# A fused attention and MLP kernel: key pieces in pairs, two h units ahead of the third column, and mixed blocks for the last tile but one

## The chip, the cores and the metric

The kernel runs on one core of one Trainium2 chip. The metric is the device time of one execution in microseconds (us). The recorder gives two numbers for each execution: the time, and the span from the first to the last recorded instruction, which is 1.8 us shorter (1196.1 against 1194.3 for the kernel before).

## The reference, cut to what matters

```python
def _attn_ref(u, v, z):                       # u, v: 8 x 3008 x 256, z: 8 x 3008 x 64
    scores = (1.0 / S) * np.matmul(z, z.transpose(0, 2, 1))
    attn = np.maximum(scores, 0.0) ** 2
    return (u * np.matmul(attn, v)).astype(np.float32)

def _moe_ref(x, w_in, w_out):                 # x: 24064 x 256, w_in: 256 x 2048, w_out: 2048 x 256
    h = x @ w_in
    g = h * np.cos(h)
    return (g @ w_out).astype(np.float32)
```

The second function takes the output of the first as its tokens.

## The kernel before

The 24,064 tokens are 48 tiles of 512 (the last of each batch is shorter). Four engines form a pipeline. For a *column* (512 queries of the attention) TensorE multiplies scores into one of the double PSUM banks `E`, ScalarE (ACT) takes the relu, VectorE (DVE) squares it into a *key piece* `A`, and TensorE multiplies the pieces with `v` into two accumulators, one for each half of the 256 outputs: the two `M` banks and one `E` pair. `gate_sum` adds the two row groups of an accumulator (ACT copies one bank, DVE adds the other), and the gate multiplies with `u` to `x`. An *h unit* is four matmuls of x with `w_in` into an `E` bank; ACT takes the cosine `c`, DVE makes `g`. A *y block* is eight matmuls of g with `w_out` into M. From tile 1 to tile 45, y is made from seven *products* of mixed quarters in place of eight plain ones; POOL and DVE add and subtract the quarters.

The order in which the first three columns take their key pieces:

```python
    def phase_a_first(s, n, extra={}):
        ...
        pair = [E[ea][:, 0, :], E[ea][:, 1, :]]
        acc = [pair, M] if s == 1 else [M, pair]
        last = NB - 1
        steps = [
            (dh, k)
            for I in range(NC)
            for dh in range(2)
            for k in range(4 * I, min(4 * I + 4, last))
        ] + [(2, last)]
        lo, hi = 5 if s == 0 else 2, 42      # where the scores of the next column go
        ...
```

The stage that joins h of one tile with y of the tile before it:

```python
    def mixed(m):
        return 1 <= m < NSLOT - 2
    ...
    order_y = (5, 1, 6, 7, 2, 3, 4)
    ...
    def phase_b(s):
        y, hs = s - 2, [(s - 1, i) for i in (0, 4, 1, 5, 2, 6, 3, 7)]
        if s == 2:
            hs = [(0, i) for i in range(8)] + hs
        ...
        if mixed(y):
            ys = [lambda n=n: product(y, n) for n in order_y]
            ...
        else:
            ys = [lambda i=i: emit_y(y, i) for i in range(8)]
            ys[7] = lambda f=ys[7]: (f(), store_y(y))
        n = len(hs)
        if n > 8:
            after = (1, 3, 5, 7, 9, 11, 13, 14)     # y block j follows h unit after[j]
        elif mixed(y):
            ...
```

And the main sequence:

```python
    phase_a_first(0, 12, {4: lambda: turn_late(4), 8: lambda: turn_late(5)})
    phase_a_first(1, 12)
    nc.gpsimd.dma_start(w_out16, moe_w_out.rearrange("(k p) f -> p k f", p=P))
    phase_a_first(2, 14)
    ...
    phase_b(2)
    ...
    for s in range(3, NSLOT + 1):
        ...                                         # phase_a(s) and phase_b(s)
    last_y(NSLOT - 1)
```

Of the kernel before, what the change touches and what calls it, by code (L numbers as in the profile page):

```python
# [14 lines left out]
def kernel(  # L15
# [13 lines left out]
    B, S, D = u.shape  # L29
    dqk = z.shape[2]  # L30
    Dff = moe_w_in.shape[1]
    P = 128
# [3 lines left out]
    NC = (S + CW - 1) // CW  # L36
    WL = S - (NC - 1) * CW
    NFT = Dff // P
    NSLOT = B * NC
# [28 lines left out]
    s1, s2, s4 = (kpool.tile([P, NFT // 2, 2 * P], FP16, name=n) for n in ("s1", "s2", "s4"))  # L68
# [25 lines left out]
    def drop_piece(key):  # L94
        i = pieces.pop(key)
        if pending.get(i):
            pending[i] = "dropped"
        else:
            free_pieces.append(i)
# [247 lines left out]
    def phase_a_first(s, n, extra={}):  # L347
        b, J = s // NC, s % NC
        ea = e_order.pop(0)
        pair = [E[ea][:, 0, :], E[ea][:, 1, :]]  # L350
        acc = [pair, M] if s == 1 else [M, pair]
        last = NB - 1
        steps = [
            (dh, k)
            for I in range(NC)
            for dh in range(2)
            for k in range(4 * I, min(4 * I + 4, last))
        ] + [(2, last)]
        lo, hi = 5 if s == 0 else 2, 42
        at = {}  # L360
        for i in range(n):
            p = lo + (hi - lo) * i // (n - 1)
            at[p] = at.get(p, 0) + 1
        for i, (dh, k) in enumerate(steps):
            if i in extra:
                extra[i]()
            if dh == 2:
                emit_value(b, J, last, 0, 0, acc[0][0], False, True)
                emit_value(b, J, last, 1, 1, acc[1][1], False, True)
            else:  # L370
                for t in range(2):
                    emit_value(
                        b, J, k, t, dh, acc[dh][t], k == 0, k == last - 1 and t != dh
                    )
            if dh > 0 and (k % 4 == 3):
                drop_piece((b, J, k // 4))
                if s > 0:
                    emit_turns((0, 0), 1)
                    if k < 4:
                        turn_u(s)  # L380
                    elif k < 8:
                        for d in range(2):
                            gate_mul(s - 1, d, late_sums.pop(0))
            for _ in range(at.get(i, 0)):
                emit_score(later=squares if s == 0 and i == lo else None)
        if s == 0:
            turn_u(0)
        late_sums.extend(gate_sum(s, *acc[dh]) for dh in range(2))
        hold(late_sums[0][0:1, 0:1])
        load_u(s + 1)  # L390
        e_order.append(ea)
# [4 lines left out]
    def emit_h(m, i):  # L396
        W = mwidth(m)
        x = xs[m]
        e = E[take_e()]
        for f in range(2):  # L400
            ft = 2 * i + f
            for k in range(2):
                nc.tensor.matmul(  # L403
                    e[:, f, 0:W],
                    w_in16[:, k, ft * P:(ft + 1) * P],
                    x[:, k, 0:W],
                    start=(k == 0),
                    stop=(k == 1),
                )
        c = cpool.tile([P, 2, CW], FP16, name="c")  # L410
        nc.scalar.activation(c[:, :, 0:W], e[:, :, 0:W], AF.Sin, bias=half_pi, scale=inv_s2)  # L411
        if m not in gs:
            gs[m] = gpool.tile([P, NFT, CW], FP16, name="g")
        return lambda: nc.vector.scalar_tensor_tensor(  # L414
            gs[m][:, 2 * i:2 * i + 2, 0:W], e[:, :, 0:W], 1.0, c[:, :, 0:W], ALU.mult, ALU.mult
        )

    def mixed(m):
        return 1 <= m < NSLOT - 2

    F = NFT // 2
    T = 2 * P
# [12 lines left out]
    def mix_late(m, which, c):  # L435
        g, f = gs[m], slice(4 * c, 4 * c + 4)
        n, up, low = halves_of(m)
        if which == "s2":
            nc.vector.tensor_tensor(s2[:, f, 0:n], s1[:, f, 0:n], g[:, f, up], ALU.subtract)  # L439
        else:  # L440
            nc.vector.tensor_tensor(  # L441
                s4[:, f, 0:n], g[:, F + 4 * c:F + 4 * c + 4, up], s2[:, f, 0:n], ALU.subtract
            )
# [8 lines left out]
    y_outs, y_parts = {}, {}  # L452

    order_y = (5, 1, 6, 7, 2, 3, 4)
# [6 lines left out]
            )  # L461
        nc.scalar.activation(y_outs[m][0][:, 1, :], acc, AF.Copy, bias=0.0, scale=inv_s2)

    def product(m, n):
        g = gs[m]
        nk, up, low = halves_of(m)
        nk = nk // P
        t = lambda i: w_mix[:, i, :, :]
        left, right = {
            1: (g[:, 0:F, up], w_out16[:, 0:F, 0:P]),  # L470
            2: (g[:, F:, up], w_out16[:, F:, 0:P]),
            3: (s4, w_out16[:, F:, P:D]),
            4: (g[:, F:, low], t(3)),
            5: (s1, t(0)),
            6: (s2, t(1)),
            7: (g[:, 0:F, low], t(2)),
        }[n]
        at = order_y.index(n) + (nk == 1 and n in order_y[4:])
        acc = M[at % 2][:, 0:nk * P]
        for ft in range(F):  # L480
            for k in range(nk):
                nc.tensor.matmul(  # L482
                    acc[:, k * P:(k + 1) * P],
                    left[:, ft, k * P:(k + 1) * P],
                    right[:, ft, :],
                    start=(ft == 0 and k == 0),
                    stop=(ft == F - 1 and k == nk - 1),
                )
        acc = acc.rearrange("p (k d) -> p k d", d=P)
        if n == 5:  # L490
            y_outs[m] = [opool.tile([P, 2, D], FP32, name="o") for i in range(2)]
            y_parts[m] = {}
        c11, c12, c21, c22 = (y_outs[m][i][:, 0:nk, d * P:(d + 1) * P] for i in range(2) for d in range(2))
        parts = y_parts[m]
        add = lambda dst, other: nc.vector.scalar_tensor_tensor(
            dst, acc, inv_s2, other, ALU.mult, ALU.add
        )
        if n in (1, 5, 6):
            parts[n] = ypool.tile([P, 2, P], FP32, name=f"p{n}")[:, 0:nk, :]
        if n in (1, 5):  # L500
            nc.scalar.activation(parts[n], acc, AF.Copy, bias=0.0, scale=inv_s2)
        elif n == 6:
            add(parts[6], parts[1])
            nc.gpsimd.tensor_tensor(c12, parts[6], parts[5], ALU.add)
        elif n == 7:
            add(c21, parts[6])
            nc.gpsimd.tensor_tensor(c22, c21, parts[5], ALU.add)
        elif n == 2:
            add(c11, parts[1])
        elif n == 3:  # L510
            add(c12, c12)
            store_half(m, 0, y_outs[m][0])
        else:
            add(c21, c21)
            store_half(m, 1, y_outs[m][1])

    def y_bank(m, k):
        if m == NSLOT - 1 and k == 3:
            return E[0][:, 0, 0:D]
        return M[k // 2][:, (k % 2) * D:(k % 2 + 1) * D]  # L520

    def y_block(m, ft, k):
        final = m == NSLOT - 1
# [58 lines left out]
    def phase_b(s):  # L582
        y, hs = s - 2, [(s - 1, i) for i in (0, 4, 1, 5, 2, 6, 3, 7)]
        if s == 2:
            hs = [(0, i) for i in range(8)] + hs
        for dh in range(len(late_sums)):
            gate_mul(s, 2 - len(late_sums), late_sums.pop(0), nc.gpsimd)
        if mixed(y):
            ys = [lambda n=n: product(y, n) for n in order_y]
            if mwidth(y) < CW:  # L590
                ys.insert(4, lambda: middle(y))
        else:
            ys = [lambda i=i: emit_y(y, i) for i in range(8)]
            ys[7] = lambda f=ys[7]: (f(), store_y(y))
        n = len(hs)
        if n > 8:
            after = (1, 3, 5, 7, 9, 11, 13, 14)
        elif mixed(y):
            after = (0, 1, 2, 3, 4, 5, 6, 6)
        else:  # L600
            after = (0, 1, 2, 3, 4, 5, 6, 6)
        for i, (m, unit) in enumerate(hs):
            times_c = emit_h(m, unit)
            if not mixed(y):
                times_c()
            for f, place in zip(ys, after):
                if place == i:
                    f()
            if mixed(y):
                times_c()  # L610
            if mixed(m) and unit >= 4:
                mix_early(m, unit - 4)
            if i in (1, 3, 5):
                emit_turns((0, 0), 1)
# [58 lines left out]
    M = [ppool.tile([P, CW], FP32, name=f"M{i}", tag=f"M{i}") for i in range(2)]  # L673
# [26 lines left out]
    phase_a_first(0, 12, {4: lambda: turn_late(4), 8: lambda: turn_late(5)})  # L700
    phase_a_first(1, 12)
    nc.gpsimd.dma_start(w_out16, moe_w_out.rearrange("(k p) f -> p k f", p=P))
    phase_a_first(2, 14)
    assert done_groups[0] == need[3]
    emit_turns((0, 3))
# [63 lines left out]
```

## Time and profile before

| | before |
|---|---|
| time | 1197.23 us, median of 3 runs (1196.8 to 1197.61) |
| profiled run | 1196.1 us, span 1194.3 us |
| TensorE busy | 1184.6 us of the span, 99% |
| next busiest | DVE, 1008.6 us, 84% |

The prediction shows the head of the page and the stops between 36 and 56 us. Three other places are needed to follow the argument. In the timelines the columns are: start in us, duration in us, engine, line, operation, output and inputs, shapes, count; in brackets the idle time before it and what ended it. This is the timeline of TensorE of the kernel before, around 24 us, where column 1 begins:

```profile
24.47 0.59 PE L258 MATMUL M<-A,v 64*128 64x512 f16 x3 [0.28 <-DVE sm L270]
25.07 0.39 PE L194 MATMUL E<-zT 64*128 64x512 f16 x2
```

Two things wait there for the same engine: the value matmul into M, and then, in order, a score that needs an E bank. DVE's own timeline in the same window shows who lets the score go:

```profile
24.34 0.68 DVE L270 TENSOR_TENSOR sm<-E,sm 128x512 f32<-128x512 f32 x1
```

It ends at 25.02, and the score starts at 25.07. The third place is the last stage, 8 h units of tile 47 with 8 y blocks of tile 46; the first and last lines of it in the timeline of TensorE of the kernel before:

```profile
1168.92 1.03 PE L403 MATMUL E<-xodd,w_in 128*128 128x512 f16 x4
1169.79 1.04 PE L524 MATMUL M<-w_out,g 128*128 128x256 f16 x8
...
1182.82 1.36 PE L524 MATMUL M<-w_out,g 128*128 128x256 f16 x11
```

It takes 13.89 us and TensorE never stops in it.

### The profile page before, as it was taken

Reading aid. Unit: us, or ns where it says so; the run is one execution under the profiler, and the core shown is the slowest. Engines: PE = TensorE matmul, PEld = TensorE weight load, DVE = VectorE, ACT = ScalarE, POOL = GpSimd, SP = SyncE. Lnnn points to the kernel's source line nnn. Section 1 sums busy time; section 2 is a strip of 40 time slices with the busy share of each in tenths; the row PEclk is TensorE's granted clock in tenths of the full one; section 3 lists DMA queues with packets and bytes.
Section 4 is the critical chain, followed back from the end, with each engine's and each line's share of the span. In section 5 each row is a group of like instructions: output and inputs, shape, how many; then the busy total and the mean of one; then the engine's idle time right before and its main releaser. Section 6 shows DMA issues by size and latency. Waiting matters only on the chain.

```text
span 1194.3 us, 28924 instructions
## 1 busy us (share of the span) xinstructions
PE 1184.6 (99%) x11839; PEld 727.2 (61%) x11839; DVE 1008.6 (84%) x1293; ACT 795.1 (67%) x927; POOL 678.4 (57%) x707
## 2 busy tenths in 40 slices
PE   9899999999999999999999999999999999999998
PEld 4556655665566656566556665666656666665566
DVE  6798988888988898888988889888888888888775
ACT  7866666666766676666766676766766666666454
POOL 3186745557565573665647556476565765545450
PEclk9999999999999999999999999999999999999999
DMA  9999898769995699956999459974798838954301
GB/s 159 172 165 163 121 153 127 118 107 137 139 139 104 114 140 157 128 92 113 150 147 132 91 107 156 169 117 77 121 160 154 122 70 122 183 105 89 65 19 54
DMA packets 479861, 147.98 MB, mean 124 GB/s; under 512 B 404208, under 2 KB 479472, under 8 KB 479728
## 3 DMA queue, kind: packets, MB, share of 16 engines
q1 hardware_dynamic: 380752, 112.93, 54.5%
q0 software_dynamic: 97440, 32.78, 28.1%
q8 instruction: 92, 1.51, 0.5%
q10 hardware_dynamic: 1536, 0.43, 0.2%
q14 instruction: 41, 0.34, 0.1%
HBM read 66.32 MB, written 24.64 MB: 76 GB/s over the span
## 4 chain that ended last, share of the span: by engine, by line
PE 97%; ACT 1%; DVE 1%; issue 1%; ACTq 0%; DVEq 0%
PE E L403 27%; PE M L482 23%; PE M L258 20%; PE E L258 19%; PE E L194 5%; PE M L524 2%; ACT r L204 1%; PE M L459 1%; PE E L654 0%; DVE sm L270 0%; PE E L524 0%; DVE A L209 0%; DVE x L286 0%; DVE g L414 0%; PE M L677 0%
## 5 line engine op out<-in xcount | busy, mean ns | idle before, releaser
L411 ACT ACTIVATE c<-E 128x1024 f16<-128x1024 f32 (+1 forms) x384 | 385.6, 1006 | 218.0 <-PE E L403 214.8
L414 DVE SCALAR_TENSOR_TENSOR g<-E,c 128x1024 f16<-128x1024 f32 (+1 forms) x384 | 458.9, 1197 | 66.7 <-ACT c L411 65.7
L204 ACT ACTIVATE r<-E 128x512 f16<-128x512 f32 (+1 forms) x342 | 327.8, 967 | 114.1 <-PE E L194 108.4
L258 PEld LDWEIGHTS <-v 64*128 64x128 f16 x4512 | 246.8, 94 | 232.4 <-issue 20.6
L403 PE MATMUL E<-x,w_in 128*128 128x512 f16 (+1 forms) x1408 | 353.8, 375 | 0.0
L432 POOL TENSOR_TENSOR s<-g 128x512 f16<-128x512 f16 (+1 forms) x180 | 202.9, 1127 | 185.4 <-DVE g L414 138.9
L258 PE MATMUL M<-A,v 64*128 64x512 f16 (+1 forms) x2256 | 284.9, 372 | 2.1 <-ACT sm L269 1.2
L258 PE MATMUL E<-A,v 64*128 64x512 f16 (+1 forms) x2256 | 279.4, 372 | 0.0
L433 POOL TENSOR_TENSOR g<-g 128x512 f16<-128x512 f16 (+1 forms) x180 | 214.2, 1190 | 14.1
L403 PEld LDWEIGHTS <-w_in 128*128 128x128 f16 x1536 | 133.4, 98 | 108.6 <-issue 19.1
L482 PEld LDWEIGHTS <-g 128*128 128x128 f16 x2752 | 168.6, 98 | 39.8
L209 DVE TENSOR_TENSOR A<-r 128x1024 f16<-128x1024 f16 x240 | 173.3, 734 | 15.1 <-ACT r L204 14.3
L286 POOL TENSOR_TENSOR x<-sm,uT 128x512 f16<-128x512 f32 (+1 forms) x43 | 48.5, 1130 | 214.1 <-DVE sm L270 213.9
L482 PEld LDWEIGHTS <-s 128*128 128x128 f16 x2064 | 126.6, 98 | 30.6
L194 PE MATMUL E<-zT 64*128 64x512 f16 (+4 forms) x684 | 130.0, 356 | 0.5 <-ACT zT L647 0.3
L439 DVE TENSOR_TENSOR s<-s,g 128x1024 f16<-128x1024 f16 (+1 forms) x90 | 98.5, 1094 | 2.1 <-POOL s L432 2.1
L482 PE MATMUL M<-w_out,g 128*128 128x128 f16 x1376 | 91.5, 219 | 0.0
L482 PE MATMUL M<-w_mix,g 128*128 128x128 f16 x1376 | 91.5, 219 | 0.0
L482 PE MATMUL M<-w_mix,s 128*128 128x128 f16 x1376 | 91.5, 219 | 0.0
L212 DVE TENSOR_TENSOR A<-r 128x512 f16<-128x512 f16 (+1 forms) x102 | 80.7, 792 | 10.2 <-ACT r L204 9.4
L194 PEld LDWEIGHTS <-zT 64*128 64x128 f16 x684 | 39.3, 94 | 36.7 <-issue 2.2
L441 DVE TENSOR_TENSOR s<-g,s 128x1024 f16<-128x1024 f16 (+1 forms) x90 | 59.4, 662 | 0.0
(58 smaller groups left out, 657.6 us busy)
## 6 DMA issues: line engine op xcount, KB each, us to landing
out_dram<-o SPq DMA_DIRECT2D x87, 256.0 KB, 2.2
v<-in_v_dram POOLq DMA_DIRECT2D x40, 256.0 KB, 9.2
u<-in_u_dram POOLq DMA_DIRECT2D x40, 256.0 KB, 4.8
A<-A SPq DMA_TRANSPOSE x252, 5.2
z<-in_z_dram POOLq DMA_DIRECT2D x14, 192.0 KB, 10.6
z<-in_z_dram POOLq DMA_DIRECT2D x14, 176.0 KB, 6.3
v<-in_v_dram POOLq DMA_DIRECT2D x8, 192.0 KB, 12.0
u<-in_u_dram POOLq DMA_DIRECT2D x8, 192.0 KB, 4.0
```

Source lines behind the costliest of these rows:

```text
L194: nc.tensor.matmul(e[:, t, 0:Wt], zT[rows, k * P:(k + 1) * P], zT[rows, J * CW:J * CW + Wt], start=True, stop=True,)
L204: nc.scalar.activation(r[:, :, 0:W], e[:, :, 0:W], AF.Relu)
L209: nc.vector.tensor_tensor(a4, r4, r4, ALU.mult)
L212: nc.vector.tensor_tensor(a4, r[:, :, 0:W], r[:, :, 0:W], ALU.mult)
L258: nc.tensor.matmul(bank[:, 0:width(J)], vs[b, k // 4][t * H:(t + 1) * H, k % 4, dh * P:(dh + 1) * P], value_rhs(b, J, k, t), start=start, ...
L403: nc.tensor.matmul(e[:, f, 0:W], w_in16[:, k, ft * P:(ft + 1) * P], x[:, k, 0:W], start=(k == 0), stop=(k == 1),)
L411: nc.scalar.activation(c[:, :, 0:W], e[:, :, 0:W], AF.Sin, bias=half_pi, scale=inv_s2)
L414: return lambda: nc.vector.scalar_tensor_tensor(gs[m][:, 2 * i:2 * i + 2, 0:W], e[:, :, 0:W], 1.0, c[:, :, 0:W], ALU.mult, ALU.mult)
L432: nc.gpsimd.tensor_tensor(s1[:, f, 0:n], g[:, f, low], g[:, lower, low], ALU.add)
L433: nc.gpsimd.tensor_tensor(g[:, f, low], g[:, f, up], g[:, f, low], ALU.subtract)
L439: nc.vector.tensor_tensor(s2[:, f, 0:n], s1[:, f, 0:n], g[:, f, up], ALU.subtract)
L482: nc.tensor.matmul(acc[:, k * P:(k + 1) * P], left[:, ft, k * P:(k + 1) * P], right[:, ft, :], start=(ft == 0 and k == 0), stop=(ft == F - ...
```

## The change

Its intent: take away the stops of TensorE at both ends of the program. Part 1 lets each accumulator of columns 1 and 2 take eight key blocks in turn and not four, so the second accumulator is touched later. Part 2 issues two of the sixteen h units of the first joint stage ahead of column 2, where TensorE waits for the M banks. Part 3 makes y of tile 46 from seven products too. The core of the diff (cut: the plumbing that passes each product its place, and the swap of the two M banks for the last tile):

```diff
+        run = 1 if s == 0 else 2
         steps = [
             (dh, k)
-            for I in range(NC)
+            for I in range(0, NC, run)
             for dh in range(2)
-            for k in range(4 * I, min(4 * I + 4, last))
+            for k in range(4 * I, min(4 * (I + run), last))
         ] + [(2, last)]
...
     def mixed(m):
-        return 1 <= m < NSLOT - 2
+        return 1 <= m < NSLOT - 1
...
-            hs = [(0, i) for i in range(8)] + hs
+            hs = [(0, i) for i in range(2, 8)] + hs
...
-            ys = [lambda n=n: product(y, n) for n in order_y]
+            late = s == NSLOT
+            ys = [
+                lambda n=n, i=i: product(y, n, i)
+                for i, n in enumerate((1, 5) + order_y[2:] if late else order_y)
+            ]
...
-            after = (1, 3, 5, 7, 9, 11, 13, 14)
+            after = (1, 2, 4, 5, 7, 8, 10, 11)
+        elif s == NSLOT:
+            after = (0, 1, 3, 4, 5, 6, 7)
...
+            if s == NSLOT and i in (1, 3):
+                for c in range(2):
+                    mix_late(y, "s2" if i == 1 else "s4", c)
...
     phase_a_first(1, 12)
     nc.gpsimd.dma_start(w_out16, moe_w_out.rearrange("(k p) f -> p k f", p=P))
+    for i in range(2):
+        emit_h(0, i)()
     phase_a_first(2, 14)
```

More of the change, by code (lines that the diff above doesn't have):

```diff
@@ L462, in middle, with product @@
         nc.scalar.activation(y_outs[m][0][:, 1, :], acc, AF.Copy, bias=0.0, scale=inv_s2)
-    def product(m, n):
+    def product(m, n, place):
         g = gs[m]
@@ L477, in product @@
         }[n]
-        at = order_y.index(n) + (nk == 1 and n in order_y[4:])
-        acc = M[at % 2][:, 0:nk * P]
+        acc = M[(place + (nk == 1 and place >= 4)) % 2][:, 0:nk * P]
         for ft in range(F):
@@ L489, in product @@
         acc = acc.rearrange("p (k d) -> p k d", d=P)
-        if n == 5:
+        if m not in y_outs:
             y_outs[m] = [opool.tile([P, 2, D], FP32, name="o") for i in range(2)]
@@ L519, in y_bank @@
             return E[0][:, 0, 0:D]
-        return M[k // 2][:, (k % 2) * D:(k % 2 + 1) * D]
+        bank = 1 - k // 2 if m == NSLOT - 1 else k // 2
+        return M[bank][:, (k % 2) * D:(k % 2 + 1) * D]
     def y_block(m, ft, k):
```

## The prediction

> **What bounds the kernel now.** I read the page first. TensorE (PE) is busy 1184.6 of 1194.3 us and no other engine is above 84%; the chain of work that ended last says the same:
>
> ```profile
> PE 1184.6 (99%) x11839; PEld 727.2 (61%) x11839; DVE 1008.6 (84%) x1293; ACT 795.1 (67%) x927; POOL 678.4 (57%) x707
> ...
> PE 97%; ACT 1%; DVE 1%; issue 1%; ACTq 0%; DVEq 0%
> ```
>
> The reader is to see that time can come from two sources only: PE work removed, or the 9.7 us in which PE stands still. The steady middle (columns 3 to 46) is the same instruction sequence before and after, buffers aside, as a comparison of the two built programs shows. So the ends of the program decide. The timeline of PE, windows 35 to 41 and 51 to 58 us, has the two largest stops outside the start-up:
>
> ```profile
> 37.69 0.37 PE L258 MATMUL M<-A,v 64*128 64x512 f16 x1 [1.22 <-ACT sm L269]
> 38.65 0.80 PE L258 MATMUL M<-A,v 64*128 64x512 f16 x5 [0.59 <-DVE sm L270]
> ...
> 52.05 1.90 PE L403 MATMUL E<-x,w_in 128*128 128x512 f16 x8
> 55.52 1.05 PE L524 MATMUL M<-w_out,g 128*128 128x256 f16 x8 [1.58 <-DVE g L414]
> ```
>
> Column 1 ends at about 36.3 us; column 2 begins in the two M banks, which ACT (L269) and then DVE (L270) must read first. By start times PE loses 37.69-36.31 = 1.38 and 38.65-37.91 = 0.74 us, 2.1 us together. At 52.05 the first two h units of tile 0 are issued, and the first y block needs their g, which DVE has only at 55.46: 55.52-53.77 = 1.75 us lost. Matmul ends are modelled, so I count starts, not the bracketed idle time. A third, small stop is in the timeline at 74 to 76 us:
>
> ```profile
> 73.99 1.08 ACT L554 ACTIVATE o<-M 128x512 f32<-128x512 f32 x2
> 74.70 0.10 PEld L258 LDWEIGHTS <-v 64*128 64x128 f16 x2 [0.42 <-issue]
> 74.70 1.87 PE L258 MATMUL M<-A,v 64*128 64x512 f16 x12
> 75.12 0.95 PEld L258 LDWEIGHTS <-v 64*128 64x128 f16 x10 [0.33 <-issue]
> ```
>
> Column 3 writes M while ACT still copies y of tile 0 out of it (to 75.07): about 0.3 us lost.
>
> **What the Trainium skill says.** (1) "TensorE: Matmul & The Clock Gate", section "Wait — 56ns, not 53.3ns?": a warm matmul of N columns starts N/2.4 GHz + about 2.5 ns after the one before, 215.7 ns at N=512. The trace agrees: h, h, y repeats every 2.60 us (56.41, 59.01, 61.61), which is 8 x 0.2157 + 8 x 0.109. So an h unit (4 matmuls of 512) and a y block (8 of 256) each cost 0.866 us of PE, and a mixed product (16 of 128) 0.89 (h plus product repeat every 1.755 us). (2) The same page, section "The mechanism": matmuls are strict FIFO. So one blocked matmul stops all behind it, and moving an independent h unit ahead of the blocked one is a gain. (3) "SBUF — State Buffer", section "Who interferes with whom": a DVE op with two SBUF inputs contends with a GpSimd op that reads SBUF, one with a single SBUF input does not. The trace agrees: the mixing sums of L439 take 0.69 us alone and 1.64 beside POOL, while L414, which reads PSUM and c, stays at 1.22 us. That matters for part 3.
>
> **The change part by part.**
>
> *Part 1, key pieces in pairs in columns 1 and 2.* No matmul is added or removed. In column 1 (dh=0 in an E pair, dh=1 in M) M is first touched at step 8, no longer step 4. That removes the 0.28 us stop at 24.47. But the score matmul after step 5 needs an E bank that the DVE sum frees at 25.02, and it starts at 25.07 before; it is still the next thing on PE, with the same wait. So PE arrives early and stops at the same 25.07: gain 0. The reordering needs squares earlier (row piece 3 at step 20 and not 24); they land at 29.25 for a use at about 29.6 us in column 1, so I expect no new stall.
>
> *Part 2, two h units ahead of column 2.* Their inputs are there: x of tile 0 at 30.5, w_in landed at 13.98+11.2 = 25.2 us. They run from 36.31 to 38.04, inside the hole; the second M bank frees at about 38.6 as before. So 2 x 0.866 = 1.73 us of PE work vanish from after column 2. In exchange ACT has two sines (1.94 us) and DVE two g products ahead of column 2's scores. Column 2 has one E pair as accumulator, so its scores alternate on the same two E's that h used. The first can start when DVE is through with g 0: 38.6+1.2 = 39.8, not 39.09; the second at 41.0, not 39.96. ACT's chain of 14 relus, unbroken before (39.70 + 12.61), starts its second 1.0 us later; there is 0.2 to 0.3 us of slack until the narrow score at 46. I take column 2 to end 0.9 us later, at 52.95.
>
> Then two h's (units 2 and 3) to 54.7, then the first y block, whose g is long there. What it waits for now is w_out: issued at 39.31, 16.0 us to landing by the table of DMA issues, so 55.3. It begins at about 55.4, against 55.52. From there the kernel before had 14 h and 8 y, 22 x 0.866 = 19.05 us (55.52 to 74.6, as the trace shows); now it is 12 h and 8 y, 17.3 us. DVE has 14 g products at a pitch of 1.14 to 1.22 us, 16 to 17 us from 55.4, and the new spacing (three h, two y in 4.33 us) leaves it keeping up. Gain 1.73 + 0.12 = 1.85 us. The last y is now followed by two h units (1.73 us of PE) where one was, so ACT's copies of M (1.08 us) are over before column 3: gain another 0.3.
>
> *Part 3, y of tile 46 in seven products.* Before: 8 y blocks and 8 h units, 1168.92 to 1182.82 = 13.9 us. Now 8 h and 7 products: 8 x 0.866 + 7 x 0.89 = 13.16, a gain of 0.74 on PE alone. But no score column runs in this stage, so the mixing sums come inside it. Walking through it: the last g of tile 46 is ready at 1171.4, POOL's sum s1 at about 1172.6 to 1172.8, and the second product would need it at 1172.2: 0.5 us lost. DVE gets 8 g products (1.14 pitch), 4 sums (0.61), 5 additions (0.34): about 13.3 us from 1171.4 on, so DVE ends near 1185.0, just ahead of the last matmuls that need its g. PE then reaches the last tile at about 1182.6, 0.25 us earlier. The two output buffers of tile 46 are stored earlier than the last tile needs them, so the tail is unchanged. Gain 0.25.
>
> Sum: 1.85 + 0.3 + 0.25 + 0 = 2.4 us. 1197.23 - 2.4 = **1194.8 us**.
>
> **The rivals.**
> 1. *w_out lands earlier or does not gate.* If it lands before 54.7, y starts when PE gets there and the gain of part 2 is up to 2.6, the total 3.2: 1194.0. For it: transposes share the DMA engines and might move. Against: its issue is tied to the same DVE sum (38.59), and the software queue is busy until about 55.
> 2. *The E banks, not M, become the wait of column 2.* If relus stay late through the column by more than 1 us, or the two g products delay squares that column 2 multiplies with, part 2 gives back 0.5 to 1 us more: 1195.5. For it: ACT had no idle time there before. Against: y waits for w_out until 55.4 anyway, which hides the first 0.7 us.
> 3. *DVE becomes the bound of the last stage.* It had 10.68 of 13.90 us there; now it is near full. If POOL's share or the additions stretch it by 0.5 us, part 3 costs 0.3 where I gain 0.25: 1195.4.
> 4. *Column 3 runs into POOL.* POOL's mixing for tile 1 ends at about 82.7 us by its own chain, while column 3 comes 2 us earlier; DVE sums then sit beside POOL longer (1.64 for 0.69). If M or E is freed late, 0.5 to 1 us goes: 1195.5. Against: I find the second sum's input at 81.2, about when DVE gets there.
>
> **Range and chances.** All of the parts act on 50 of 1194 us, and all PE idle time outside start-up is below 5 us, so 2% (24 us) either way is out of reach short of a hang-like wait. The rivals span 1194.0 to 1196; the runs before differ by 0.8 among themselves. Range 1193.7 to 1196.3. Faster by over 2%: 0.01; within 2%: 0.98; slower: 0.01.
>
> **What would show it.** In the new profile: two L404 groups at about 36.3 without a stop before 38; the first scores of column 2 waiting for DVE at 39.8 and 41.0; the first L525 matmul at 55.4, waiting for w_out's DMA and not DVE; column 3 starting near 72.6 with no stop after its first step; the step at 25.07 unchanged; a short wait on POOL in the second product of the last stage and DVE almost full there; last-tile matmuls 2.1 + 0.25 us earlier than 1182.82. The prediction is wrong if column 2 ends past 53.7, if y starts after 56, or if the middle is not shifted by a constant of about 2.1 us.

## The result, and the profile after

| | before | after |
|---|---|---|
| time, median (range), 4 runs each | 1197.01 us (1196.61 to 1197.61) | 1193.32 us (1192.88 to 1193.59) |
| profiled run | 1196.1 us, span 1194.3 | 1193.15 us, span 1191.4 |

The ratio is 0.9968, 95% interval 0.9951 to 0.9986. It is "same" by the 2% line, as predicted, but the time lies 0.4 us below the range and the median moved by 3.7 us, not 2.4.

The head of the page of the changed kernel:

```profile
PE 1183.3 (99%) x11887; PEld 727.2 (61%) x11887; DVE 1012.3 (85%) x1302; ACT 794.9 (67%) x927; POOL 690.5 (58%) x717
...
PE 97%; ACT 1%; DVE 1%; issue 0%; POOL 0%; DVEq 0%; ACTq 0%
```

48 more matmuls, 1.3 us less busy time on TensorE, and the same engine ends last. The spans differ by 2.95 us, so by this count more than half of the gain is stops taken away and not work; as matmul ends are modelled, the starts below decide. The timeline of TensorE of the changed kernel in the hole that the prediction is about:

```profile
36.30 1.90 PE L404 MATMUL E<-x,w_in 128*128 128x512 f16 x8
38.13 1.21 PE L258 MATMUL M<-A,v 64*128 64x512 f16 x6
39.77 0.39 PE L194 MATMUL E<-zT 64*128 64x512 f16 x2 [0.43 <-DVE g L415]
...
40.90 0.39 PE L194 MATMUL E<-zT 64*128 64x512 f16 x2
```

The eight h matmuls fill the hole; the price is the scores at 39.77 and 40.90 (39.09 and 39.96 before), which wait for the g products. Behind column 2, in the same view:

```profile
52.77 1.90 PE L404 MATMUL E<-x,w_in 128*128 128x512 f16 x8
54.51 1.04 PE L525 MATMUL M<-w_out,g 128*128 128x256 f16 x8
```

The first y block follows the two h units with no bracket, so with no stop: 54.51 - 52.77 is two h units of 0.87. Before, the same two lines stood at 52.05 and 55.52. The weights `w_out` that this block needs were issued at 39.2 and had landed at 54.1, just in time (view of the tile `w_out`, changed kernel):

```profile
L712 POOL DMA_DIRECT2D w_out<-in_moe_w_out_dram x1: 1159/1159/1159, 39.2 to 39.2; - x1
...
DMA to landing us min/median/max: 14.9/14.9/14.9
```

Where column 3 begins, ACT's copies of y are now done before TensorE comes (timeline of all engines, changed kernel):

```profile
70.37 1.08 ACT L555 ACTIVATE o<-M 128x512 f32<-128x512 f32 x2
71.95 1.47 PE L258 MATMUL M<-A,v 64*128 64x512 f16 x12
```

The score near 25 us still waits for the same sum of DVE, only its bracket is longer, as the work ahead of it went faster:

```profile
24.96 0.39 PE L194 MATMUL E<-zT 64*128 64x512 f16 x2 [0.66 <-DVE sm L270]
```

And the last stage has two new stops (timeline of TensorE, changed kernel):

```profile
1168.64 0.83 PE L482 MATMUL M<-w_mix,s 128*128 128x128 f16 x12
1169.80 0.40 PE L482 MATMUL M<-w_mix,s 128*128 128x128 f16 x4 [0.32 <-POOL s L433]
1170.03 1.89 PE L404 MATMUL E<-xodd,w_in 128*128 128x512 f16 x8
1171.78 1.22 PE L482 MATMUL M<-w_mix,s 128*128 128x128 f16 x16
1172.84 1.03 PE L404 MATMUL E<-xodd,w_in 128*128 128x512 f16 x4
```

A product of 16 matmuls takes 0.89 us where nothing stops it. The first shown here, which is the second product of the stage, takes 1.39 (to 1170.03), the next 1.06 (to 1172.84): 0.5 and 0.17 us lost.

Cutting both traces at the start of the same matmuls gives where the time went:

| stretch, by starts of matmuls | before | after | difference |
|---|---|---|---|
| to the score near 25 us | 25.07 | 24.96 | -0.11 |
| columns 1 and 2, to the h units after column 2 | 26.98 | 27.81 | +0.83 |
| to the first y block | 3.48 | 1.74 | -1.74 |
| to column 3 | 19.18 | 17.44 | -1.74 |
| column 3 | 11.63 | 11.23 | -0.40 |
| first h after column 3 to first h after column 4 | 25.08 | 25.34 | +0.26 |
| from there to the last stage | 1057.51 | 1057.51 | 0 |
| last stage | 13.89 | 13.84 | -0.05 |
| sum | | | -2.95 |

The two profiled runs differ by 1196.1 - 1193.15 = 2.95 us as well, so nothing is left over between them. But the medians differ by 3.7. The sum of the prediction was 2.4. There were thus two questions: which terms were mis-sized in the pair of traces (0.55 us), and why the medians differ by 0.7 us more than the traces.

### The profile page after: what moved, and what is told of

Same layout as the page of the kernel before. It is cut to its first block, busy times and chain, and to the rows that moved or that the text cites. A ratio compares the mean times of both kernels' runs of the same rounds, so it can differ in the third digit from the quotient of the medians. Undisturbed runs are those within 1.5% of the kernel's fastest.

```text
span 1191.4 us, 29044 instructions
## 1 busy us (share of the span) xinstructions
PE 1183.3 (99%) x11887; PEld 727.2 (61%) x11887; DVE 1012.3 (85%) x1302; ACT 794.9 (67%) x927; POOL 690.5 (58%) x717
## 4 chain that ended last, share of the span: by engine, by line
PE 97%; ACT 1%; DVE 1%; issue 0%; POOL 0%; DVEq 0%; ACTq 0%
PE E L404 27%; PE M L482 23%; PE M L258 20%; PE E L258 19%; PE E L194 5%; PE M L525 1%; ACT r L204 1%; PE M L460 1%; DVE g L415 0%; PE E L664 0%; DVE sm L270 0%; PE E L525 0%; POOL s L433 0%; ACT c L412 0%; DVE o L495 0%
## 5 line engine op out<-in xcount | busy, mean ns | idle before, releaser
L433 POOL TENSOR_TENSOR s<-g 128x512 f16<-128x512 f16 (+1 forms) x184 | 208.3, 1132 | 188.5 <-DVE g L415 138.7
L434 POOL TENSOR_TENSOR g<-g 128x512 f16<-128x512 f16 (+1 forms) x184 | 219.5, 1193 | 14.4
L482 PEld LDWEIGHTS <-g 128*128 128x128 f16 x2816 | 172.5, 98 | 40.8
L482 PEld LDWEIGHTS <-s 128*128 128x128 f16 x2112 | 129.4, 98 | 32.1 <-DVE s L440 0.5
L194 PE MATMUL E<-zT 64*128 64x512 f16 (+4 forms) x684 | 127.6, 355 | 2.0 <-DVE sm L270 0.7
L482 PE MATMUL M<-w_mix,s 128*128 128x128 f16 x1408 | 94.0, 219 | 0.3 <-POOL s L433 0.3
```

What stands on the lines that cost most here:

```text
L194: nc.tensor.matmul(e[:, t, 0:Wt], zT[rows, k * P:(k + 1) * P], zT[rows, J * CW:J * CW + Wt], start=True, stop=True,)
L433: nc.gpsimd.tensor_tensor(s1[:, f, 0:n], g[:, f, low], g[:, lower, low], ALU.add)
L434: nc.gpsimd.tensor_tensor(g[:, f, low], g[:, f, up], g[:, f, low], ALU.subtract)
L482: nc.tensor.matmul(acc[:, k * P:(k + 1) * P], left[:, ft, k * P:(k + 1) * P], right[:, ft, :], start=(ft == 0 and k == 0), stop=(ft == F - ...
```

## The experiments

Fourteen runs of ten kernels were made in four sets, each set on one chip beside runs of the kernel before. All outputs are right. The traces repeat to about 0.02 us in most stretches; what varies from run to run is the start, the landing of `w_out`, and one thing that the first set brought up.

### Each part alone, and the change again

`p1_only` has only the first hunk of the diff (`run`). `p2_only` has only the two h units, their removal from the later list, and the new `after`. `p3_only` is the changed kernel with those two parts undone. `after_again` is the changed kernel.

> Key pieces in pairs alone (part 1). Theory A (the gain is the two h units in the hole, as the two traces show it): 0, within 0.2 us of before; the score matmul near 25 us still waits for the DVE sum, and the first y block still waits for g near 55.5. Rival B (the new order of the pieces moves the transposes and so the landing of w_out, and that made the part of the gain that I had not foreseen): still 0 here, since g gates y as well, but w_out lands at about 54.1 and not at 55.3. Rival C (part 1 removes a stop of its own): 0.3 to 0.7 us faster.

> Two h units ahead of column 2 and the new spacing alone (part 2). Theory A: nearly the whole gain, 2.7 to 3.7 us, and the first y block starts at about 54.5 us with w_out landed before it. Rival B: w_out lands at about 55.3 as in the trace of before, the first y block waits for it, and the gain is 0.7 to 0.9 us smaller than that of the whole change.

> y of the last but one tile in seven products alone (part 3). Theory A (the stage lost in waits on POOL and DVE what it gained in matmuls): 0 to 0.2 us faster, with the wait of 0.5 us on POOL in the second product and 0.35 us on the DVE sum in the third. Rival: 0.7 us faster, as the matmul count says, the difference in the profiles of the pair being chance.

> The changed kernel unchanged, on the same chip as the three others. The spans of the first pair of profiles differ by 2.9 us and the timed medians by 3.7. Theory A: the middle is the same to 0.01 us in all runs, so that the difference is chance in when the first inputs and w_out arrive; several spans of both kernels give 3.0 to 3.6 us. Rival: a gain of 3.7 us or more, which would mean that the profile of before was a lucky run in which a wait was shorter than usual.

| | median us (range), 5 runs | ratio to before, 95% |
|---|---|---|
| before, 9 runs | 1197.57 (1195.87 to 1198.22) | |
| p1_only | 1197.66 (1195.91 to 1197.77) | 0.9996 (0.9982 to 1.0009) |
| p2_only | 1193.09 (1193.01 to 1194.78) | 0.9968 (0.9956 to 0.9981) |
| p3_only | 1196.16 (1195.86 to 1196.46) | 0.999 (0.9977 to 1.0002) |
| after_again | 1193.46 (1192.88 to 1194.53) | 0.9969 (0.9957 to 0.9982) |

Part 2 alone gives the whole gain. Part 1 gives nothing: the score near 25 us starts at 25.05 in its trace, and column 1, from its first value matmul to its last, takes 13.38 us there as in the kernel before. Part 3 makes the last stage 13.84 us, as in the changed kernel, and leaves all stretches ahead of it as before; its median looks 1.4 us better only because all five of its runs lie in the lower of the two groups, about 1.5 us apart, into which the runs of the kernel before fall, so that is no effect of it.

Two surprises. First, in `after_again` the first y block came at 56.05 and not 54.51 (timeline of TensorE):

```profile
52.98 1.90 PE L404 MATMUL E<-x,w_in 128*128 128x512 f16 x8
56.05 1.05 PE L525 MATMUL M<-w_out,g 128*128 128x256 f16 x8 [1.17 <-ACT c L412]
```

The bracket names ACT, whose cosine was long done; the table of transfers has `w_out` landing 16.6 us after its issue at 39.4, at 56.0. So it is the transfer. Second, `p1_only` changes nothing near 40 us, and yet its stretch "columns 1 and 2" took 28.51 us and not 26.98. The windows view shows why. The columns are the stretch, its length, the busy time (instructions) of PE, PEld (weight loads), DVE, ACT and POOL, the granted clock (the share of TensorE's full speed that the trace records), the DMA share and GB/s. The kernel before:

```profile
36.00:39.00 3.00, 1.20 (x11) 0.41 (x7) 2.21 (x4) 1.64 (x3) 0.60 (x2) 1.00 1.22 216
39.40:43.20 3.80, 3.80 (x39) 2.14 (x36) 2.00 (x3) 3.50 (x4) 1.07 (x1) 1.00 0.99 124
```

The trace of `p1_only`:

```profile
36.00:39.00 3.00, 1.20 (x10) 0.41 (x7) 2.19 (x4) 1.61 (x3) 0.63 (x2) 1.00 1.23 212
39.40:43.20 3.80, 3.80 (x24) 1.70 (x20) 1.39 (x2) 2.23 (x3) 1.05 (x1) 0.55 0.99 132
```

TensorE is as busy, but does 24 matmuls where 39 went, at a mean clock of 0.55. The recorded grant is 0.5 for one interval of 3413 ns, from 39.6 to 43.0 us. It comes right behind the hole at 36 to 38.6, where TensorE did almost nothing (1.20 us of 3.00: the end of column 1, one matmul at 37.67, and the first of column 2 from 38.62). Value matmuls start 0.43 us apart in it and not 0.215, and the stretch is 1.53 us longer. So a new theory, called H: **the hole of the kernel before makes the clock halve for one interval in some of its runs, and the h units that fill the hole also take this away.** Its rival R: those slower runs have some other cause, and the changed kernel has them as well.

### Is the hole to blame for the slower runs?

`before_look`, `before_look2` and `before_look3` are the kernel before, to catch the slower group in a trace. `before_fill` and `before_fill2` are the kernel before with eight matmuls of no use in the hole:

```diff
+    for i in range(8):
+        nc.tensor.matmul(E[e_order[0]][:, 0, :], warm[:, 0:P], warm, start=True, stop=True)
     phase_a_first(2, 14)
```

> The kernel before with eight matmuls of zeros (8 x 0.216 = 1.73 us, results never read) in the hole between columns 1 and 2, and nothing else. They do no useful work and fit into a stop that is there anyway. Theory H (the hole of 2.3 us lets the throttle halve the clock for one window of 3.4 us in about two runs of three, as the trace of part 1 alone shows from 39.6 to 43.0; that costs 1.5 us and makes the upper group of the spans of before, 1195.8 to 1196.4 beside 1194.1 to 1194.8): all spans in the lower group, median 1196.0 to 1196.5, so 1.0 to 1.5 us faster than before. Rival R (the two groups come from when w_out or the first inputs land): the same as before within 0.3 us, with both groups still there.

> The kernel before again, for its trace only. Theory H: if its span is above 1195.5 us, its trace shows matmuls at half rate for 3.4 us after the hole at 36 to 38.6 us; if it is below 1195, it shows none. Rival R: a long span without such a stretch, its first y block later than 55.5 us and behind w_out.

> The kernel before, for its trace. Theory H: a span above 1195.7 us shows matmuls at half rate for 3.4 us after the hole near 36 to 38.6 us, and the stage from the score at 25 to the first h unit takes 28.5 us and not 26.98; a span below shows 26.98. Rival R: a long span with 26.98 us in that stage.

> As the look before: Theory H: a span above 1195.7 us with 28.5 us from the score at 25 to the first h unit, or a span below with 26.98. Rival R: a long span with 26.98.

> The kernel before with the eight idle matmuls in the hole, again: the first time the before runs beside it were nearly all in the lower group (8 of 11), so that nothing could be gained, and one run of 1200.8 us spoilt the mean. Theory H (the hole causes the halved clock): no span between 1195.7 and 1196.6 us; in ten runs of the two jobs at most the lone far one, against 8 of 29 in before. Rival R (the halved clock comes whatever is in the hole): 2 of 5 spans in the upper group.

`before_look` (span 1194.7 us) and `before_look3` (1194.6) fell in the lower group, with no throttled interval. `before_look2` (1197.46 us, span 1195.7): its windows view reads like that of `p1_only`, and nothing in the kernel differs from the profiled run of before:

```profile
36.00:39.00 3.00, 1.20 (x11) 0.42 (x8) 1.99 (x4) 1.42 (x3) 0.82 (x2) 1.00 1.24 214
39.40:43.20 3.80, 3.80 (x24) 1.68 (x20) 1.39 (x2) 2.48 (x3) 0.85 (x1) 0.55 0.98 126
```

All its other stretches agree with before to 0.01 us; columns 1 and 2 take 28.51 for 26.98. In the two traces of the slower group that exist, the halved clock thus makes the difference. All six traces of kernels with the hole open fit: two with a halved interval and spans of 1195.7 and 1195.9, four without and spans of 1194.1 to 1194.7.

In the four sets, 12 of 38 runs of the kernel before have a span of 1195.6 or more (5 of 9, 3 of 11, 0 of 9 and 4 of 9). With the hole filled by useless matmuls, none of 10 runs lies there (the highest is at 1195.5, just short of it), against 7 of 20 runs of before beside them; an eleventh run of `before_fill`, at a span of 1200.8 us, is unexplained. No median moved: `before_fill` 1196.79 us (1196.25 to 1202.65) for 1196.4 of before, ratio 1.0008 (0.9993 to 1.0024); `before_fill2` 1196.65 (1196.49 to 1196.75) for 1196.63, ratio 0.9998 (0.9985 to 1.001). Where the expectation was that the median would fall, it was missed: most runs of before are in the lower group anyway, so the median sits there; what the filling changed is the upper end of the range, 1196.75 for 1197.74 us in the second set. For H speak the traces and the missing upper group; the counts alone are too few to prove it. None of the eight traces with h units in the hole has the interval.

The record holds two more checks. It gives the mean granted clock of every run, traced or not. One halved interval loses 1.7 us of clock, so a run that has one can't be listed at 1.000. All 12 long runs of the kernel before are listed at 0.999 or 0.998; of the 26 others, 23 are at 1.000. This is a sign and no proof, as some clock is also lost behind the last matmul (up to 1.2 us in the traces). The filled run at 1195.5 is at 1.000, so it has no halved interval. The one at 1200.8 is at 0.997, a loss of 3 us or more: either its clock halved although the hole was filled, or its end was long; no trace shows which.

The second check is where the stop lies. In every trace the full clock is first granted between 3.9 and 7.2 us, and both halved intervals begin ten steps of 3.413 us after that; so the steps can be counted off in all traces. The stop lasts 2.34 us and begins between 36.1 and 36.7. In the two halved traces it lies whole within one step (36.19 to 39.60 in `p1_only`, 36.04 to 39.45 in `before_look2`). In the four others with the hole open, a step ends inside the stop (at 37.07, 37.94, 37.02 and 38.08; in the last, `p3_only`, 2.0 us of the stop lay in one step, and the clock stayed full). In `before_fill` (step 35.80 to 39.21) and four traces with h units in the hole (`after`, `after_third`, `after_late_order`, `best`), a step covers the place whole, matmuls fill it, and the clock stays full. An estimate from these figures: if the steps fall evenly, a stop of 2.34 us lies whole within one in (3.41 - 2.34) / 3.41 = 31% of the runs, and 12 of 38 is 32%. So where the stop falls among the steps seems to decide whether a run is slow. This fits all eleven traces, but no run set the position on purpose.

### Does w_out gate the first y block?

`after_wout_early` issues the load one column earlier:

```diff
+    nc.gpsimd.dma_start(w_out16, moe_w_out.rearrange("(k p) f -> p k f", p=P))
     phase_a_first(1, 12)
-    nc.gpsimd.dma_start(w_out16, moe_w_out.rearrange("(k p) f -> p k f", p=P))
```

`after_third` is the changed kernel a third time, to see whether its runs ever show the halved clock or the wait.

> The changed kernel with w_out issued one column earlier, right after column 0. In the changed kernel w_out landed at 54.1, 54.9 (part 2 alone) and 56.0 us in three profiles, and the first y block, ready at about 54.5, waited 0.0, 0.4 and 1.5 us for it. Theory: w_out lands before 50 us, no wait, and the upper runs (1194.4 to 1194.8) are gone: median 1192.9 to 1193.2, all runs within 0.8 us. Rival (the upper runs come from elsewhere, or the earlier transfer delays the transposes or v): same or slower, spread as before.

> The changed kernel again, so that three jobs show how often it waits for w_out. Theory: spans of 1191.1 to 1191.8 without the wait, up to 1193.0 with it (1 to 2 of 5), none with the halved clock in column 2. Rival: the long spans come from a halved clock here too, and the trace, if it is a long one, shows it.

`after_wout_early`: 1193.14 us (1192.86 to 1193.27), ratio 0.997 (0.9958 to 0.9982), spans 1191.0 to 1191.5. Its load lands after 11.3 us, long before it is needed, and the first y block follows 1.74 us after the h units. `after_third`: 1193.05 us (1192.82 to 1193.76), ratio 0.9967 (0.9953 to 0.998); its trace (span 1192.0) names the wait outright, in the timeline of TensorE:

```profile
52.96 1.90 PE L404 MATMUL E<-x,w_in 128*128 128x512 f16 x8
55.34 1.05 PE L525 MATMUL M<-w_out,g 128*128 128x256 f16 x8 [0.48 <-DMA w_out<-in_moe_w_out_dram]
```

So the wait that the prediction named exists, but not in every run. In the fourteen traces with the load in its old place it lands 14.1 to 16.6 us after issue; of six with the h units ahead, three wait for it (`p2_only` 0.3, `after_third` 0.64, `after_again` 1.3 us) and three do not. Taking it away cost nothing here and makes runs alike; the median hardly moves (the changed kernel's lie between 1193.05 and 1193.46).

### What the seven products gave back

`after_late_order` keeps the seven products of the last stage, but orders them so that those which need the sums of POOL and DVE come later:

```diff
-                for i, n in enumerate((1, 5) + order_y[2:] if late else order_y)
+                for i, n in enumerate((1, 2, 5, 6, 7, 3, 4) if late else order_y)
...
-            after = (0, 1, 3, 4, 5, 6, 7)
+            after = (0, 1, 2, 4, 5, 6, 7)
```

> The changed kernel with another order of the seven products of tile 46: the two that need no mixed block first, the sums later (1, 2, 5, 6, 7, 3, 4, the empty place after the fourth h unit). Theory (part 3 gained 0.06 instead of 0.74 us because the second and third product wait 0.5 us for POOL and 0.3 us for DVE): these waits vanish and the stage is 0.6 to 0.8 us shorter; median 0.5 to 0.8 us below the changed kernel. Rival (DVE is the bound of this stage, at 10.7 us of g products, 2.6 of sums and 1.7 of additions in 13.9): no gain, the wait appears in front of the last tile's matmuls.

It ran 1192.88 us (1192.31 to 1193.38), ratio 0.9969 (0.9956 to 0.9982); the last stage is 13.30 us, 0.54 less than with the changed kernel's order. That is somewhat less than the 0.6 to 0.8 us expected, and the median is 0.2 to 0.6 us below those of the changed kernel, taken in other sets. Its timeline of TensorE has, where the two stops were, none:

```profile
1170.00 1.06 PE L482 MATMUL M<-w_mix,s 128*128 128x128 f16 x16
1170.89 1.89 PE L404 MATMUL E<-xodd,w_in 128*128 128x512 f16 x8
1172.62 1.06 PE L482 MATMUL M<-w_mix,s 128*128 128x128 f16 x16
1173.51 1.03 PE L404 MATMUL E<-xodd,w_in 128*128 128x512 f16 x4
```

Both products take 0.89 us. So the work saved by the seven products is real, and the order gave it back. The wait for POOL was the reason and not, as rival 3 had it, DVE as the bound of the stage: DVE has the same work here and the stage is shorter. DVE is now close to being the bound, though: the windows view has it busy for 12.85 us of the 13.30.

### What column 3 gained

The second matmul of the first pair of column 3 starts 0.42 us after the first in before (ACT still copies M), at once in the changed kernel. `after_old_space` puts the last two y blocks later, so that the copies end later:

```diff
-            after = (1, 2, 4, 5, 7, 8, 10, 11)
+            after = (1, 3, 5, 7, 9, 11, 12, 12)
```

> The changed kernel with the y blocks of tile 0 spaced as before (one after every second h unit), so that only one h unit follows the last y block. By the stages of its trace: Theory (the new spacing saves the stop at the start of column 3, in which the second of two paired matmuls waits 0.42 us for ACT's copy of M and the pairs stay apart to the end of the column): column 3 takes 11.6 us again and not 11.22, all other stages as in the changed kernel. Rival (column 3 is shorter because DVE is less behind): 11.2 us.

It ran 1193.03 us (one look, span 1191.2). The copies now end 0.1 us after column 3 starts (timeline of all engines):

```profile
70.91 1.08 ACT L555 ACTIVATE o<-M 128x512 f32<-128x512 f32 x2 [0.51 <-PE M L525]
...
71.88 1.61 PE L258 MATMUL M<-A,v 64*128 64x512 f16 x12
```

The second matmul trails by 0.16 us, and column 3 takes 11.37 us, between the 11.63 of before and the 11.22 of the changed kernel. That was between theory and rival, as the copies ended sooner than I had reckoned. The three points lie on one line: the length of the column is 11.21 us plus the lag of that first pair (0.42, 0.16, 0). The lag is never made up within the column.

### A version with three more changes

`best` is the changed kernel with the early load, the mended order, and the scores of columns 1 and 2 a few steps later, so that fewer of them wait for a bank:

```diff
-        lo, hi = 5 if s == 0 else 2, 42
+        lo, hi = (5, 4, 5)[s], 42
```

> The changed kernel with three mends that the runs point to: w_out issued after column 0; the seven products in the order 1, 2, 5, 6, 7, 3, 4; and the scores of columns 1 and 2 begun at step 4 and 5 and not at step 2, so that values fill the stops in front of them (1.04 us before the score at 25, 0.8 and 0.47 us before the scores at 39.8 and 40.9). Theory: 0.54 us from the products as measured alone, 0.4 to 0.7 in column 1, 0.4 to 0.7 in column 2, no waits for w_out: median 1191.2 to 1192.0, about 1.5 us below the changed kernel. Rival (ACT's chain of relus is the bound of columns 1 and 2, so that later scores only move the stop): 0.5 us from the products alone, median 1192.5.

It ran 1192.05 us (1191.69 to 1192.54), ratio to before 0.9965 (0.9952 to 0.9979), beside 1196.31 us (1195.91 to 1196.59) of before in a set in which before had no slow-group run. Its median is 1.0 to 1.4 us below the three medians of the changed kernel (1193.05 to 1193.46), taken in other sets; as before had no slow-group run here, the ratios hardly differ (0.9965 for 0.9967 to 0.9969). That it is faster than the changed kernel rests on the stages of its trace: 0.57 us in columns 1 and 2 (27.24 for 27.81) and 0.53 us in the last stage. It just missed its expectation: column 1 gained 0.36 and column 2 0.20 us, where 0.4 to 0.7 each were expected. Its timeline of TensorE shows what is left:

```profile
39.30 0.44 PE L194 MATMUL E<-zT 64*128 64x512 f16 x2
39.51 0.66 PE L258 MATMUL M<-A,v 64*128 64x512 f16 x4
40.43 0.39 PE L194 MATMUL E<-zT 64*128 64x512 f16 x2 [0.26 <-DVE g L415]
```

The first score now comes without a wait, the second still waits for the second g product.

## Why the prediction was right or wrong

| term | predicted | measured (profiled pair) | comment |
|---|---|---|---|
| part 1, score near 25 us | 0 | -0.11 | start-up, which varies by 0.6 us between traces |
| columns 1 and 2 | +0.9 | +0.83 | right |
| to the first y block | -1.02 (wait for w_out to 55.4) | -1.74 | **failed**: no wait, y at 54.51 |
| 12 h and 8 y in place of 14 and 8 | -1.73 | -1.74 | right |
| column 3 | -0.3 | -0.40 | lag of the first pair |
| after column 3 to after column 4 | 0 | +0.26 | column 4's first matmul waits for DVE |
| last stage | -0.25 | -0.05 | two stops in place of one |
| sum | -2.4 | -2.95 | |
| halved clock behind the hole | not thought of | up to -1.53 in the runs that have it | **missing** |

**Right.** TensorE bounds the kernel before and after; the middle is unchanged to 0.01 us, so what the ends gain arrives whole at the end. Part 1 gains nothing, for the reason given. The h units fit the hole without a stop. Column 2 pays with two scores that wait for the g products (39.77 and 40.90 for the predicted 39.8 and 41.0) and ends 0.7 us later at 52.77, for 52.95 predicted. The second product of the last stage waits for POOL as named.

**The step that failed** is "What it waits for now is w_out: issued at 39.31, 16.0 us to landing by the table of DMA issues, so 55.3. It begins at about 55.4". The duration of one transfer in one trace was taken as a constant, although other transfers ran beside it (1.8 MB on the transposes' queue between 38 and 58 us of the kernel before). In the profiled run it took 14.9 us from 39.2, landed at 54.1, and y never waited; over the traces the same program waited 0 to 1.3 us. This was rival 1, for which the text had put 1194.0; of its arguments against, "its issue is tied to the same DVE sum" concerns the issue and not the spread of the landing, and "the software queue is busy until about 55" was again read from one trace.

**The step that was missing** is the start of the sum. The prediction subtracts a gain read from one profiled run (1196.1 us) from a median of other runs (1197.23). The 1.1 us between the two was never asked about. In the sets run later such a difference comes from the group of long runs, those with a halved interval behind the hole as far as traces show it, and part 2 takes it away along with the hole. How much of the first four runs of before was of that kind can't be told, as they left no traces; by their times, one of 1197.61 lies where such runs lie, and one of 1197.23 between the groups. So the 0.7 us by which the medians differ more than the traces is explained in kind, and its size is argued and not shown. None of the rivals had it: all four asked what else could wait, and none what a stop itself brings about. The sentence that shut it out is "time can come from two sources only: PE work removed, or the 9.7 us in which PE stands still". In a halved interval TensorE counts as busy (3.80 of 3.80 us) and does 24 matmuls where 39 went: a third source.

The measured median, 1193.3 us, is 1.5 us below the predicted 1194.8. Of this, 1.1 us is the start of the sum (1197.23 against 1196.1) and 0.55 us its terms: `w_out` alone makes 0.72, and the small gains and losses in the table partly cancel. The median after lies 0.17 us above its profiled run, which takes that much off. So neither failed step alone explains the miss.

**Smaller.** Column 3 gained the full lag of its first pair, 0.42, where 0.3 was put by eye. In the last stage the waits came to 0.67 us against 0.74 us of saved work; the wait for POOL was sized right (0.5), the further 0.17 us was not foreseen. Column 4 lost 0.26 us in the traces of the changed kernel and of `p2_only`, waiting for a DVE addition (L495), and lost nothing in the others; why only there stays open. Also open are the 1200.8 us run of `before_fill` and how long a stop must be for the clock to halve (here 2.0 us within one step did not do it, and 2.3 us did).

## What to carry to other kernels

Before subtracting a gain from a median, ask whether the profiled run lies where the median lies; if not, the profile lacks something that the other runs have, and a look at a slower run costs little. A stop of TensorE may cost more than itself (here one of 2.3 us cost 1.5 us more in about a third of the runs), so filling it with useful work from later can be worth more than its length. A transfer's landing time from one trace is one draw: where it gates something by a fraction of a us, issue it earlier and the question goes away.

## What the Trainium skill lacked or had wrong

- "TensorE: Matmul & The Clock Gate", section "What's actually happening", puts the half clock "after ≥1 idle window (~3.4µs)". The windows of 3413 ns are seen here too, as the length of the halved interval. But here no whole window was idle: a stop of 2.3 us with one matmul inside it was enough, in 12 of 38 runs by their spans, and in two other runs whose traces show it. It cost 1.53 us in both traces. The page calls the window free-running, and in the eleven traces compared above the clock halved just where the stop lay whole inside one window and was not filled; no run set that position.
- The same page, section "The mechanism" of row packing, shows two row groups starting 4 ns apart. It says nothing of what happens when the second starts late: here a lag of 0.42 or 0.16 us at the first pair of a column lengthened the whole column by just that (11.63 and 11.37 us for 11.22).
- "DMA: Bandwidth & Descriptors", section "Anatomy of one DMA — SWDGE (gpsimd) path", gives one fit for a transfer's time and no spread. The same load of `w_out` took 14.1 to 16.6 us from issue to landing beside other transfers in fourteen traces, and 11.3 and 11.4 us in the two traces where it was issued a column earlier.
